# Retention and a mixture of experts on one core: weight pieces loaded and cast a block earlier, choices and gathers reordered

## The chip, the cores and the metric

One core of a Trainium2 chip runs the whole kernel as one program. The metric is device time in microseconds, the median of several runs. The engines are TensorE (PE), VectorE (DVE), ScalarE (ACT), GpSimd (POOL) and SyncE (SP); SP issues the plain transfers, POOL the indirect ones, and each engine works through its program in order, waiting on semaphores.

## The reference

Attention is a retention with a decay per head; its output is the input of a top-1 mixture of experts.

```python
gamma = 1.0 - 2.0 ** (-5.0 - np.arange(H))
for t in range(S):                       # B, H, S, D = 4, 8, 768, 64
    state = gamma * state + einsum('bhd,bhe->bhde', k[:, :, t], v[:, :, t])
    y[:, :, t] = scale * einsum('bhd,bhde->bhe', q[:, :, t], state)
x = y.transpose(0, 2, 1, 3).reshape(B * S, H * D)          # 3072 rows of 512
logits = normalized(x) @ normalized(expert_emb).T / tau    # 8 experts
e = argmax(logits); gate = softmax(logits)[e]
out = gate * (relu(x @ w1[e]) @ w2[e])                     # w1: 512 x 1024, w2: 1024 x 512
```

## The kernel before

The retention runs in 12 blocks of 256 positions (`m` from 0 to 11, `NM` is 12; three blocks make one batch). A block has scores q.k (L381), a mask on DVE (L401), products of q with the running state (`inter`, L444), products of the masked scores with v (`intra`, L444), and products that carry the state on (L415). In the same turn the next block is got ready: POOL scales k and q two blocks ahead (`scale_k` L344, `scale_q` L339), PE transposes them (L350, L368) and ACT copies the transposes out of PSUM (`kT` L355, `qT` L369). `take(m)` (L460, L463, ACT) copies a block's result out of the two `py` banks, of which there is one pair, so that the next block's `inter` must wait for it. DVE turns the result into rows (`rows_turn`, L468) and SP writes them to the scratch `xd` in DRAM (L475, four writes of 128 KB).

Beside this runs the routing. `logits_products` and `logits_rows` (L488, L496) give a block's logits; for a group of blocks (`GROUPS`) `sums` and `choose` find the expert of each row (L506 to L526, result `oh`), `add_counts` and `count` count rows per expert (L533 to L546), `ranks` gives each row its slot (L553 to L557, result `sloti`), and `place` writes a 16-word entry per row into the table `tbl` in DRAM, by one indirect transfer of POOL per 128 rows (L566). Block 8 is a group by itself, so that after block 9 the first 18 columns of the table (`NBE`) are known; `pad` (L582, L585) makes the later rows of expert 0 begin at slot 288. Then `early_slots` (L602, SP) loads the first 288 entries of expert 0, POOL turns their indices to integers (L590) and gathers the rows into `xge` (L596) in block 10. Block 9's rows and the next weight loads on SP are held until this gather has landed.

Expert weights come in pieces of 512 KB, eight per expert (`load_piece`, into one of four `raw` buffers); the first four pieces of expert 0 are each four transfers of 128 KB (L192), the others one (L194, L198). `split_cast` casts a piece on ACT into its high part (L219), and the function it gives back computes the low part on DVE (L224). In the kernel before, pieces 0 and 1 are loaded at the end of block 8, 2 and 3 in block 9, 4 and 5 in block 10; pieces 0 and 1 are cast ahead of block 9's `take`, 2 and 3 at the start of block 10.

After block 11 expert 0 runs on its early rows (`run`, L237, first layer), while the last group is counted, sorted and placed, the late entries of expert 0 are loaded (L937) and its late rows gathered into `xr0` (L596; the trace calls it `xr`), and PE transposes them (L1094). The other experts follow, each with its own gathers, first layer (L237) and second layer (L1024, L1072). The order on every engine is the order in which the code calls these functions. Where a transfer must come later than its data would allow, `after` adds a dependence.

Of the kernel before, what the change touches and what calls it, by code (L numbers as in the profile page):

```python
# [15 lines left out]
I32 = mybir.dt.int32  # L16
# [34 lines left out]
NBE = 2 * 9  # L51
SW = 16
FILL = 512
LOADS = (8, 8)
STRIDE = 3200
NOV = (NT - OV + P - 1) // P
NONE = 2 * NT
# [48 lines left out]
def retention_moe(ctx: ExitStack, tc: tile.TileContext, q, k, v, emb, tau, w1, w2, const, const16, out):  # L106
# [392 lines left out]
    def span(g):  # L499
        return slice(2 * GROUPS[g][0], 2 * GROUPS[g][-1] + 2)  # L500
# [72 lines left out]
    def run_all(*gs):  # L573
        gs = list(gs)
        while gs:
            gs = [g for g in gs if next(g, gs) is not gs]
# [10 lines left out]
                op0=ALU.is_gt, op1=ALU.add)  # L587

    def indices(p, e, c):
        nc.gpsimd.tensor_scalar(out=gi[:p, e, c], in0=tb[:p, e, c, 0], scalar1=float(NT - 1), scalar2=None, op0=ALU.min)  # L590

    def tokens(p, e, c):
        nc.gpsimd.tensor_copy(out=si[:p, e, c], in_=tb[:p, e, c, 1])

    def gather(xr, n, j, e, at, rows_=NT):
        return nc.gpsimd.indirect_dma_start(  # L596
            out=xr[:n, j, :], out_offset=None, in_=xd[:rows_, :],
            in_offset=bass.IndirectOffsetOnAxis(ap=gi[:n, e, at:at + 1], axis=0),
            bounds_check=rows_ - 1, oob_is_err=False)

    def early_slots():
        nc.sync.dma_start(out=tb[:, 0, :3], in_=tbl[:3 * P, :2 + NE].rearrange("(j p) o -> p j o", p=P))  # L602

    def early_gather():
        indices(P, 0, slice(0, 3))
        for j, n in EROWS:
            i = gather(xge, n, j, 0, j, NBE * P)
        tokens(P, 0, slice(0, 3))
        return i

# [125 lines left out]
    nc.gpsimd.memset(ze, 0.0)  # L736
    nc.gpsimd.memset(zt[:, :, 2 + NE:], 0.0)
    none = ap_.tile([P, NE * FILL // P * SW], F32, name="parts")
    nc.gpsimd.memset(none, float(NONE))
    for s in range(2):  # L740
        scale_q(0, s, nc.vector)
    transpose_q(0, 0)
# [19 lines left out]
    for m in range(NM):  # L762
        nxt = m + 1 < NM
        done = last_of.get(m - 1)
        if waiting is not None:
            pr = count(waiting)
            if span(waiting).stop == NBE:
                pad()
            run_all(ranks(waiting, pr))
            ready += range(span(waiting).start, span(waiting).stop)  # L770
        py_of(m)
        if m == NM - 2:
            first, lows = lows, [split_cast(), split_cast()]
            for u in range(2):
                spread_v(m + 1, u)

# [5 lines left out]
        if m == NM - 2:  # L782
            place(ready)
            ready = []
        if m == 0:
            for j in (*load_q(2), load_k(2)):
                after(j, i)
            nc.sync.dma_start(out=cst2, in_=const[:, _C1:])
            nc.sync.dma_start(out=tri, in_=const16)

        if m + 2 < NM:
            for s in range(2):
                after(scale_k(m + 2, s), i)
            for s in range(2):
                after(scale_q(m + 2, s), i)
        if m == 2:
            nc.gpsimd.tensor_copy(out=zt[:, :, :2], in_=C("ids").rearrange("p (n o) -> p n o", o=2))
        place(ready[:n])
        del ready[:n]
        if m == NM - 3:  # L800
            load_piece()
            load_piece()
        if m == NM - 2:
            early_slots()
            gathered = early_gather()
# [3 lines left out]
        if m == 0:  # L809
            state(0)  # L810
            state_copy(0)
            state_sums(0)
            intra(0, 0)
            intra(0, 1)
            transpose_k(1, 0)
            i = transpose_k(1, 1)
            after(load_v(2), i)
            inter(0)
            transpose_q(1, 0)
            i = transpose_q(1, 1)  # L820
            for j in (*load_q(3), load_k(3), load_v(3)):
                after(j, i)
            state(1)
            state_copy(1)
            state_sums(1)
        else:
            inter(m)
            if nxt:
                i = state(m + 1)
                state_copy(m + 1)  # L830
                if m + 3 < NM:
                    after(load_k(m + 3), i)
            if m == 2:
                after(nc.sync.dma_start(
                    out=tbl.rearrange("(e s) c -> e (s c)", e=NE)[:, :FILL * SW].rearrange("e (p x) -> e p x", p=P // NE),
                    in_=none), i)
            for i in () if m < 3 else (0, 1, 2) if m == 3 else (m - 1,):
                logits_rows(i, logits_products(i))
            if nxt:
                state_sums(m + 1)  # L840
                spread_v(m, 1, nc.vector.tensor_copy)
                transpose_k(m + 1, 0)
                transpose_q(m + 1, 0)
                i = transpose_q(m + 1, 1)
                if m + 3 < NM:
                    after(load_v(m + 3), i)
                transpose_k(m + 1, 1)
                rows(m - 1, gathered if m == NM - 2 else None)
                if m == NM - 2:
                    for low in first:  # L850
                        low()
                    load_piece(gathered)
                    load_piece(gathered)
                if done is not None:
                    z = sums(done)
                    run_all(choose(done, z))
                    run_all(add_counts(done))
                intra(m, 0)
                intra(m, 1)
            else:  # L860
                for low in lows:
                    low()
                intra(m, 0)
                z = sums(done)
                run_all(choose(done, z))
                run_all(add_counts(done))
                intra(m, 1)
                ps = [turn_rows(xge, EROWS, kt, bank(f"pst{kt}")) for kt in range(2)]
                pr = count(done)
                run_all(ranks(done, pr))  # L870
                place(range(span(done).start, span(done).stop))
        waiting = done
        if m == NM - 3:
            lows = [split_cast(), split_cast()]
        take(m)
        if m < NM - 2:
            spread_v(m + 1, 0)
        if m < 3:
            next(emb_steps)
        if m == NM - 1:  # L880
# [51 lines left out]
    for _ in range(9):  # L932
        next(sort_steps)
        run(1)
    load_expert(1)
    load_expert(2)
    nc.sync.dma_start(out=tb[:, 0, 3], in_=tbl[EARLY:CAPS[0], :2 + NE])  # L937
    slots(1)
    slots(2)
    run(10)  # L940
    split()
    run(12)
    split()
    for j, n in EROWS:
        square(xge, n, j, j)
    run(12)
    split()
    for _ in range(4):
        load_piece()
    run(DF)  # L950
    ctxa.close()
    turn_of[:] = ["b2", "b3"]
# [124 lines left out]
    yt0 = mp.tile([P, NXC, KT, Q], F32, name="yt", bufs=2)  # L1077
    og0 = mp.tile([P, NG, DM], F32, name="og", bufs=2)
    xr0 = mp.tile([P, 1, DM], F32, name="xr0")
    indices(P, 0, slice(3, 4))  # L1080
    gather(xr0, P, 0, 0, 3)
    indices(P, 1, slice(0, NG))
    gather_rows(1)
    tokens(P, 0, slice(3, 4))
# [183 lines left out]
    with ExitStack() as cx:  # L1268
# [3 lines left out]
        def expert_rows(e, i):  # L1272
# [7 lines left out]
            nc.sync.dma_start(out=mt, in_=tbl[ds(i * P + (e * STRIDE + OV), P), :])  # L1280
            g1 = op.tile([P, 1], I32, name="g1")
            s1 = op.tile([P, 1], I32, name="s1")
            nc.vector.tensor_scalar(out=g1, in0=mt[:, :1], scalar1=float(NT - 1), scalar2=None, op0=ALU.min)
            nc.vector.tensor_copy(out=s1, in_=mt[:, 1:2])
            xg = op.tile([P, 1, DM], F32, name="xg")
            nc.gpsimd.indirect_dma_start(
                out=xg[:, 0, :], out_offset=None, in_=xd[:, :],
# [23 lines left out]
        with tc.If(any_over > 0):  # L1311

            none = op.tile([P, SW], F32, name="none")
            nc.gpsimd.memset(none, float(NONE))
            nx = op.tile([P, NE], F32, name="nx")
            nc.vector.scalar_tensor_tensor(out=nx, in0=C("order"), scalar=float(STRIDE), in1=cnt, op0=ALU.mult, op1=ALU.add)
            nxi = op.tile([P, NE], I32, name="nxi")
# [36 lines left out]
```

## Time and profile before

| what | before |
|---|---|
| median of 3 runs | 403.92 us (402.48 to 404.23) |
| the profiled execution | 404.24 us, its span 402.5 us |
| PE busy | 386.1 us, 96% of the span |
| DVE, ACT, POOL busy | 254.1, 213.4, 150.9 us |
| granted clock of PE, mean | 0.997 |
| moved by DMA | 88.41 MB, 220 GB/s in the mean |

The span runs from the first to the last instruction; times in the rows below are microseconds from its start. A row of an order of time gives start, duration, engine, line, operation and tiles, and in brackets the idle time in front of it and what ended that. A count behind a tile (x32) means so many instructions merged into one row. "Idle" is worth time only on an engine that the end waits for.

### The profile page before, as it was taken

How to read it: one execution, taken by the hardware profiler on the slowest of the kernel's cores; microseconds unless marked ns; L12 is line 12 of the kernel's file. 1: busy time of each engine (PE TensorE's matmuls, PEld its weight loads, DVE VectorE, ACT ScalarE, POOL GpSimd, SP SyncE). 2: the span in 40 equal slices, each digit the busy share in tenths (PEclk: the TensorE clock that was granted, in tenths of full speed). 3: DMA queues.
4: the chain of work that ended last, by engine and by line, in shares of the span. 5: the costliest groups of instructions: out<-in, count | busy, mean ns of one | idle time of the engine just before them, and what ended most of it. 6: DMA issues, size and time to landing. Idle time of an engine off the chain costs nothing.

```text
span 402.5 us, 9525 instructions
## 1 busy us (share of the span) xinstructions
PE 386.1 (96%) x3646; PEld 355.2 (88%) x3646; DVE 254.1 (63%) x539; ACT 213.4 (53%) x378; POOL 150.9 (37%) x171
## 2 busy tenths in 40 slices
PE   6999999999899999999999999999999999999993
PEld 3998788887779978999999999999889889999972
DVE  5497867877889638854863864757456456485400
ACT  3575557565945356555544736725665445463410
POOL 2575487687445522402502611420371062001131
PEclk9999999999999999999999999999999999999998
DMA  7899979889448779589879797787888977933121
GB/s 228 262 287 254 277 225 280 235 229 260 104 130 258 234 263 265 161 267 249 266 223 247 241 302 175 246 277 221 236 273 298 190 240 225 246 122 107 31 99 54
DMA packets 88479, 88.41 MB, mean 220 GB/s; under 512 B 10803, under 2 KB 66995, under 8 KB 88424
## 3 DMA queue, kind: packets, MB, share of 16 engines
q1 hardware_dynamic: 83176, 74.60, 65.4%
q0 software_dynamic: 5072, 13.05, 9.6%
q8 instruction: 30, 0.49, 0.5%
q14 instruction: 25, 0.20, 0.2%
q10 hardware_dynamic: 176, 0.07, 0.1%
HBM read 65.01 MB, written 18.79 MB: 208 GB/s over the span
## 4 chain that ended last, share of the span: by engine, by line
PE 62%; DMA 15%; DVE 7%; issue 5%; SPq 5%; POOL 2%; ACT 2%; POOLq 0%; DVEq 0%
PE pst L237 10%; PE b L237 8%; PE py L1024 8%; PE py L237 8%; PE b L1024 5%; DMA xd<-x 5%; PE pst L1024 4%; PE b L1072 4%; PE py L1072 4%; DMA wlo<-in_k_dram 3%; SPq L1036 2%; DVE x L468 2%; PE b L381 2%; DMA xr<-xd,gi 2%; SPq L475 2%
## 5 line engine op out<-in xcount | busy, mean ns | idle before, releaser
L224 DVE TENSOR_TENSOR wlo<-raw,whi 128x1024 fp32r<-128x1024 f32 x64 | 77.8, 1218 | 23.2 <-ACT whi L219 18.3
L1054 POOL DMA_INDIRECT out_dram<-og,si x28 | 29.3, 1047 | 119.0 <-ACT og L1047 84.2
L219 ACT CAST whi<-raw 128x1024 fp32r<-128x1024 f32 x64 | 66.3, 1044 | 4.7 <-DMA raw<-in_moe_w_dram 4.6
L596 POOL DMA_INDIRECT xr<-xd,gi x25 | 29.3, 1171 | 17.5 <-issue 15.1
L401 DVE TENSOR_TENSOR pm<-b,mask 128x512 f32<-128x512 f32 x48 | 29.8, 681 | 8.9 <-PE b L381 8.9
L344 POOL TENSOR_TENSOR hl<-wlo,cst 128x512 f32<-128x512 f32 x22 | 22.6, 1049 | 31.5 <-DMA wlo<-in_k_dram 17.4
L237 PE MATMUL pst<-xl,whi 128*128 128x380 f32 (+7 forms) x96 | 32.1, 335 | 0.0
L237 PE MATMUL pst<-xh,whi 128*128 128x380 f32 (+7 forms) x96 | 32.0, 334 | 0.0
L237 PE MATMUL pst<-xh,wlo 128*128 128x380 f32 (+7 forms) x96 | 32.0, 333 | 0.0
L1005 DVE STREAM_TRANSPOSE xt<-xg 128x384 f32<-128x384 f32 (+1 forms) x28 | 15.7, 578 | 25.8 <-DMA xg<-xs 25.7
L263 POOL TENSOR_TENSOR r<-r,half 128x4 f32<-128x4 f32 (+1 forms) x9 | 8.9, 991 | 54.1 <-DVE r L262 54.1
L566 POOL DMA_INDIRECT tbl<-zt,sloti x24 | 24.2, 1009 | 12.6 <-issue 5.4
L243 ACT ACTIVATE hh<-pst 128x380 fp32r<-128x380 f32 (+7 forms) x24 | 11.6, 485 | 31.6 <-PE pst L237 31.6
L381 PE MATMUL b<-qT,kT 64*128 64x128 f32 x384 | 24.9, 279 | 2.4 <-ACT kT L355 1.5
L1006 ACT CAST xh<-xt 128x408 fp32r<-128x408 f32 (+6 forms) x28 | 14.2, 510 | 24.1 <-DVE xt L1005 23.8
L237 PE MATMUL b<-xh,whi 128*128 128x408 f32 (+7 forms) x80 | 26.7, 334 | 0.0
L237 PE MATMUL b<-xl,whi 128*128 128x408 f32 (+7 forms) x80 | 26.7, 333 | 0.0
L237 PE MATMUL b<-xh,wlo 128*128 128x408 f32 (+7 forms) x80 | 26.6, 332 | 0.0
L237 PE MATMUL py<-xh,whi 128*128 128x288 f32 (+7 forms) x80 | 26.3, 329 | 0.0
L237 PE MATMUL py<-xh,wlo 128*128 128x288 f32 (+7 forms) x80 | 26.2, 328 | 0.0
L237 PE MATMUL py<-xl,whi 128*128 128x288 f32 (+7 forms) x80 | 26.2, 327 | 0.0
L381 PEld LDWEIGHTS b<-qT,kT 64*128 64x128 f32 x384 | 22.5, 188 | 3.9 <-ACT kT L355 2.8
(220 smaller groups left out, 1044.2 us busy)
## 6 DMA issues: line engine op xcount, KB each, us to landing
raw<-in_moe_w_dram SPq DMA_DIRECT2D x60, 512.0 KB, 4.4
whi<-in_q_dram SPq DMA_DIRECT2D x24, 256.0 KB, 4.0
xd<-x SPq DMA_DIRECT2D x48, 128.0 KB, 4.2
wlo<-in_k_dram SPq DMA_DIRECT2D x11, 512.0 KB
xs<-xr SPq DMA_DIRECT2D x6, 768.0 KB, 4.8
whi<-in_v_dram SPq DMA_DIRECT2D x6, 512.0 KB
wlo<-in_v_dram SPq DMA_DIRECT2D x6, 512.0 KB, 6.0
xg<-xs SPq DMA_DIRECT2D x16, 192.0 KB, 4.6
```

What stands on the lines that cost most here:

```text
L219: nc.scalar.copy(out=hv, in_=rv)
L224: eng.tensor_tensor(out=lv, in0=rv, in1=hv.bitcast(F32), op=ALU.subtract)
L237: nc.tensor.matmul(acc[:, :w], a[:, f], x[:, kt, cols], start=(n == 0), stop=(n == 3 * KT - 1))
L344: return eng.tensor_tensor(out=ks_r[:, m % 3, s, h], in0=kin[m % 3][:, h, s], in1=w[:, h], op=ALU.mult)
L381: nc.tensor.matmul(psc[a][:, j], kTs[m][a * D:(a + 1) * D, j, u].rearrange("p s c -> p (s c)"), q_cols(m, a, j, u), start=True, stop=True, ...
L401: o.append(nc.vector.tensor_tensor(out=pm, in0=psc[a], in1=w, op=ALU.mult))
L566: i = nc.gpsimd.indirect_dma_start(out=tbl[:, :], out_offset=bass.IndirectOffsetOnAxis(ap=sloti[:, n:n + 1], axis=0), in_=zt[:, n], in_off ...
L596: return nc.gpsimd.indirect_dma_start(out=xr[:n, j, :], out_offset=None, in_=xd[:rows_, :], in_offset=bass.IndirectOffsetOnAxis(ap=gi[:n, ...
L1005: nc.vector.transpose(out=xt[:, :n], in_=xgs[e][:, :n, kt * Q:(kt + 1) * Q])
L1024: nc.tensor.matmul(acc[:, :c], a[:, f], x[:, kt, :c], start=(n == 0), stop=(n == 3 * FT - 1))
L1054: i = nc.gpsimd.indirect_dma_start(out=out[:, :], out_offset=bass.IndirectOffsetOnAxis(ap=si[:n, e, j:j + 1], axis=0), in_=og[:n, j, :], i ...
L1072: nc.tensor.matmul(acc[:s, :], x[:, kt, at], a, start=(n == 0), stop=(n == 3 * FT - 1))
```

## The change

Eight things change; `NM - 2` is block 10, `NM - 3` block 9, `NM - 4` block 8.

1. Pieces 0 and 1 are loaded at the end of block 7 and pieces 2 and 3 at the end of block 8, none in block 9.
2. Pieces 0 and 1 are cast at the end of block 8, behind its `take` and a copy of v, and 2 and 3 ahead of block 9's `take`, none in block 10. The low part of piece 0 stands ahead of block 9's logits on DVE, that of piece 1 where both stood.
3. In block 9 the choice and counts of group 3 stand ahead of the row transposes, and in block 10 the ranks ahead of `pad`.
4. q of block 11 is scaled in block 10 behind the placements, not in block 9 ahead of them.
5. The table's first two words are integers, written as such.
6. The gathers of expert 0 take their offsets from the loaded table itself; its index steps (L590) are gone, and entries without a row are out of bounds and skipped. `xr0` is cleared by a memset first.
7. Two of the four pieces that stood behind expert 0's last casts are loaded earlier, ahead of the loads of the late table.
8. The same integer entries are used in the code for overflowing experts, which does not run here.

```diff
--- before.py
+++ after.py
-LOADS = (8, 8)
+LOADS = (7, 7, 8, 8)
...
-    def gather(xr, n, j, e, at, rows_=NT):
+    def gather(xr, n, j, e, at, rows_=NT, idx=None):
...
-            in_offset=bass.IndirectOffsetOnAxis(ap=gi[:n, e, at:at + 1], axis=0),
+            in_offset=bass.IndirectOffsetOnAxis(ap=gi[:n, e, at:at + 1] if idx is None else idx, axis=0),
...
     def early_gather():
-        indices(P, 0, slice(0, 3))
         for j, n in EROWS:
-            i = gather(xge, n, j, 0, j, NBE * P)
+            i = gather(xge, n, j, 0, j, NBE * P, tb[:n, 0, j, :1].bitcast(I32))
         tokens(P, 0, slice(0, 3))
...
             pr = count(waiting)
+            run_all(ranks(waiting, pr))
             if span(waiting).stop == NBE:
                 pad()
-            run_all(ranks(waiting, pr))
...
         if m == NM - 2:
-            first, lows = lows, [split_cast(), split_cast()]
             for u in range(2):
                 spread_v(m + 1, u)
...
         if m == NM - 2:
             place(ready)
             ready = []
+            for s in range(2):
+                scale_q(m + 1, s)
...
-            for s in range(2):
+            for s in range(2 if m < NM - 3 else 0):
                 after(scale_q(m + 2, s), i)
...
-        if m == NM - 3:
-            load_piece()
-            load_piece()
...
+            if m == NM - 2:
+                lows.pop(0)()
             for i in () if m < 3 else (0, 1, 2) if m == 3 else (m - 1,):
                 logits_rows(i, logits_products(i))
...
+                if m == NM - 3:
+                    z = sums(done)
+                    run_all(choose(done, z))
+                    run_all(add_counts(done))
                 rows(m - 1, gathered if m == NM - 2 else None)
                 if m == NM - 2:
-                    for low in first:
-                        low()
+                    lows.pop(0)()
                     load_piece(gathered)
                     load_piece(gathered)
-                if done is not None:
+                if done is not None and m != NM - 3:
...
         if m == NM - 3:
-            lows = [split_cast(), split_cast()]
+            lows += [split_cast(), split_cast()]
         take(m)
         if m < NM - 2:
             spread_v(m + 1, 0)
+        if m == NM - 4:
+            lows = [split_cast(), split_cast()]
...
     load_expert(1)
+    load_piece()
+    run(10)
+    split()
+    load_piece()
     load_expert(2)
     nc.sync.dma_start(out=tb[:, 0, 3], in_=tbl[EARLY:CAPS[0], :2 + NE])
     slots(1)
     slots(2)
-    run(10)
-    split()
     run(12)
...
-    for _ in range(4):
-        load_piece()
+    load_piece()
+    load_piece()
...
     xr0 = mp.tile([P, 1, DM], F32, name="xr0")
-    indices(P, 0, slice(3, 4))
-    gather(xr0, P, 0, 0, 3)
+    nc.gpsimd.memset(xr0, 0.0)
+    gather(xr0, P, 0, 0, 3, idx=tb[:, 0, 3, :1].bitcast(I32))
```

On SP, from block 6's rows to block 8's rows (L475 rows, L327 q, L322 k and v of block 11, L192 chunks of the first pieces, L602 the early table), before:

```order
L475 DMA xd<-x 256x1x128 x4
L327 DMA whi<-in_q_dram 128x1x512 x2
L322 DMA wlo<-in_k_dram 128x8x128
L322 DMA wlo<-in_v_dram 128x8x128
L475 DMA xd<-x 256x1x128 x4
L192 DMA raw<-in_moe_w_dram 32x1024 x16
L475 DMA xd<-x 256x1x128 x4
```

and now:

```order
L475 DMA xd<-x 256x1x128 x4
L192 DMA raw<-in_moe_w_dram 32x1024 x8
L327 DMA whi<-in_q_dram 128x1x512 x2
L322 DMA wlo<-in_k_dram 128x8x128
L322 DMA wlo<-in_v_dram 128x8x128
L475 DMA xd<-x 256x1x128 x4
L192 DMA raw<-in_moe_w_dram 32x1024 x8
L475 DMA xd<-x 256x1x128 x4
```

The first eight chunks moved ahead of the loads for block 11; the second eight stay between block 7's and block 8's rows.

On ACT, from the copy of v behind block 8's `take` to block 10's copies of v (L219 casts, L460 and L463 block 9's `take`), before:

```order
L394 COPY vs<-wlo 64x512 x2
L422 COPY tB<-pst_1579 128x256
L355 COPY kT<-b_1830 128x8x64
L369 COPY qT<-b_1838 128x512
L369 COPY qT<-b_1844 128x512
L355 COPY kT<-b_1850 128x8x64
L219 CAST whi<-raw 128x1024 x2
L460 COPY yT<-py_1719 128x4x128
L463 COPY yT<-py_1720 64x4x128 x2
L394 COPY vs<-whi 64x512 x2
L219 CAST whi<-raw 128x1024 x2
L394 COPY vs<-wlo 64x512 x4
```

and now:

```order
L394 COPY vs<-wlo 64x512 x2
L219 CAST whi<-raw 128x1024 x2
L422 COPY tB<-pst_1589 128x256
L355 COPY kT<-b_1834 128x8x64
L369 COPY qT<-b_1842 128x512
L369 COPY qT<-b_1848 128x512
L355 COPY kT<-b_1854 128x8x64
L219 CAST whi<-raw 128x1024 x2
L460 COPY yT<-py_1735 128x4x128
L463 COPY yT<-py_1736 64x4x128 x2
L394 COPY vs<-whi 64x512 x2
L394 COPY vs<-wlo 64x512 x4
```

Two casts moved from block 10 to the end of block 8; two still stand ahead of block 9's `take`, and these are now pieces 2 and 3.

On POOL, from block 9's scaling to the early gather (L344 scale_k, L339 scale_q of block 11, L566 placements, four of block 9's and the two of group 3), before:

```order
L344 TENSOR_TENSOR hl<-wlo,cst_60 128x512 x2
L339 TENSOR_TENSOR hh<-whi,cst_60 128x8x64 x2
L566 DMA tbl<-zt,sloti 25600x16 x6
L590 TENSOR_SCALAR gi<-tb 128x3
L596 DMA xge<-xd,gi 128x512 x2
L596 DMA xge<-xd,gi 32x512
```

and now:

```order
L344 TENSOR_TENSOR hl<-wlo,cst_60 128x512 x2
L566 DMA tbl<-zt,sloti 25600x16 x6
L339 TENSOR_TENSOR hh<-whi,cst_60 128x8x64 x2
L596 DMA xge<-xd,tb 128x512 x2
L596 DMA xge<-xd,tb 32x512
```

The scaling of q moved behind the six placements, and the index step is gone.

## Rows read from the trace of the kernel before

**Rows 1.** The page, its first part: busy time, share of the span and instructions.

```profile
PE 386.1 (96%) x3646; PEld 355.2 (88%) x3646; DVE 254.1 (63%) x539; ACT 213.4 (53%) x378; POOL 150.9 (37%) x171
```

**Rows 2.** Busy time by stretches: PE, PEld, DVE, ACT, POOL; clock, DMA share, GB/s.

```profile
85.00:120.00 35.00, 31.66 (x538) 25.81 (x534) 28.79 (x74) 24.32 (x42) 20.21 (x21) 1.00 0.66 173
...
200.00:280.00 80.00, 80.00 (x449) 80.00 (x448) 50.63 (x102) 42.52 (x74) 19.61 (x21) 1.00 0.81 245
```

**Rows 3.** PE in order of time, block 10, block 11 and the late transposes.

```profile
99.59 0.17 PE L535 MATMUL b<-oh,tri 128*128 128x16 f16 x1 [0.67 <-DVE oh L526]
...
102.47 1.51 PE L444 MATMUL py<-qT,s 64*64 64x128 f32 x30
...
106.01 1.04 PE L368 MATMUL b<-ident,hh 128*128 128x128 f32 x8
...
107.41 1.97 PE L444 MATMUL py<-pm,vs 128*64 128x128 f32 x32
110.83 2.06 PE L381 MATMUL b<-qT,kT 64*128 64x128 f32 x32 [1.45 <-ACT kT L355]
...
116.67 1.16 PE L614 MATMUL pst<-ident,xge 128*128 128x128 f32 x6
...
143.47 0.66 PE L1094 MATMUL b<-ident,xr 128*128 128x128 f32 x4 [0.99 <-DMA xr<-xd,gi]
```

**Rows 4.** ACT in order of time, end of block 9 and block 10.

```profile
100.22 1.05 ACT L219 CAST whi<-raw 128x1024 fp32r<-128x1024 f32 x1 [0.98 <-DMA raw<-in_moe_w_dram]
101.17 0.58 ACT L460 COPY yT<-py 128x512 f32<-128x512 f32 x1
...
104.24 2.00 ACT L219 CAST whi<-raw 128x1024 fp32r<-128x1024 f32 x2
106.14 2.50 ACT L394 COPY vs<-wlo 64x512 f32<-64x512 f32 x4
```

**Rows 5.** SP's transfers in order of time: start and time to issue.

```profile
84.10 1.88 SPq L327 DMA_DIRECT2D whi<-in_q_dram  x2
86.07 0.54 SPq L322 DMA_DIRECT2D wlo<-in_k_dram  x1
...
89.08 3.19 SPq L475 DMA_DIRECT2D xd<-x  x4
92.31 8.33 SPq L192 DMA_DIRECT2D raw<-in_moe_w_dram  x16
...
116.19 2.52 SPq L475 DMA_DIRECT2D xd<-x  x4
...
134.06 2.18 SPq L194 DMA_DIRECT2D raw<-in_moe_w_dram  x4
```

**Rows 6.** Issue to landing: weight chunks (90 to 104), then the early gathers.

```profile
DMA to landing us min/median/max: 3.9/4.0/4.1
...
DMA to landing us min/median/max: 3.4/3.4/3.4
```

**Rows 7.** The chain that ended last: start, duration, what.

```profile
89.08 5.29 DMA xd<-x
94.39 2.94 DMA raw<-in_moe_w_dram
...
135.37 8.05 DMA xr<-xd,gi
```

**Rows 8.** POOL in order of time, blocks 9 and 10 and the late table.

```profile
92.53 2.04 POOL L344 TENSOR_TENSOR hl<-wlo,cst 128x512 f32<-128x512 f32 x2 [1.80 <-DMA wlo<-in_k_dram]
...
103.18 0.97 POOL L566 DMA_INDIRECT tbl<-zt,sloti  x1 [0.30 <-issue]
108.89 0.95 POOL L590 TENSOR_SCALAR gi<-tb 128x3 int32<-128x3 f32 x1 [4.74 <-DMA tb<-tbl]
...
133.98 1.12 POOL L590 TENSOR_SCALAR gi<-tb 128x1 int32<-128x1 f32 x1 [5.57 <-DMA tb<-tbl]
```

**Rows 9.** DVE in order of time, block 10.

```profile
105.65 0.45 DVE L496 STREAM_TRANSPOSE parts<-b 128x256 f32<-128x256 f32 x1 [1.63 <-PE b L488]
```

More of the change, by code (lines that the diff above doesn't have):

```diff
@@ L589, in indices @@
     def indices(p, e, c):
-        nc.gpsimd.tensor_scalar(out=gi[:p, e, c], in0=tb[:p, e, c, 0], scalar1=float(NT - 1), scalar2=None, op0=ALU.min)
+        nc.gpsimd.tensor_scalar(out=gi[:p, e, c], in0=tb[:p, e, c, 0].bitcast(I32), scalar1=float(NT - 1), scalar2=None, op0=ALU.min)
     def tokens(p, e, c):
-        nc.gpsimd.tensor_copy(out=si[:p, e, c], in_=tb[:p, e, c, 1])
-    def gather(xr, n, j, e, at, rows_=NT):
+        nc.gpsimd.tensor_copy(out=si[:p, e, c], in_=tb[:p, e, c, 1].bitcast(I32))
+    def gather(xr, n, j, e, at, rows_=NT, idx=None):
         return nc.gpsimd.indirect_dma_start(
             out=xr[:n, j, :], out_offset=None, in_=xd[:rows_, :],
-            in_offset=bass.IndirectOffsetOnAxis(ap=gi[:n, e, at:at + 1], axis=0),
+            in_offset=bass.IndirectOffsetOnAxis(ap=gi[:n, e, at:at + 1] if idx is None else idx, axis=0),
             bounds_check=rows_ - 1, oob_is_err=False)
@@ L738, in retention_moe @@
     none = ap_.tile([P, NE * FILL // P * SW], F32, name="parts")
-    nc.gpsimd.memset(none, float(NONE))
+    nc.gpsimd.memset(none.bitcast(I32), NONE)
     for s in range(2):
@@ L793, in retention_moe @@
                 after(scale_k(m + 2, s), i)
-            for s in range(2):
+            for s in range(2 if m < NM - 3 else 0):
                 after(scale_q(m + 2, s), i)
         if m == 2:
-            nc.gpsimd.tensor_copy(out=zt[:, :, :2], in_=C("ids").rearrange("p (n o) -> p n o", o=2))
+            nc.gpsimd.tensor_copy(out=zt[:, :, :2].bitcast(I32), in_=C("ids").rearrange("p (n o) -> p n o", o=2))
         place(ready[:n])
         del ready[:n]
-        if m == NM - 3:
-            load_piece()
-            load_piece()
         if m == NM - 2:
@@ L1282, in expert_rows @@
             s1 = op.tile([P, 1], I32, name="s1")
-            nc.vector.tensor_scalar(out=g1, in0=mt[:, :1], scalar1=float(NT - 1), scalar2=None, op0=ALU.min)
-            nc.vector.tensor_copy(out=s1, in_=mt[:, 1:2])
+            nc.vector.tensor_scalar(out=g1, in0=mt[:, :1].bitcast(I32), scalar1=float(NT - 1), scalar2=None, op0=ALU.min)
+            nc.vector.tensor_copy(out=s1, in_=mt[:, 1:2].bitcast(I32))
             xg = op.tile([P, 1, DM], F32, name="xg")
@@ L1313, in retention_moe @@
             none = op.tile([P, SW], F32, name="none")
-            nc.gpsimd.memset(none, float(NONE))
+            nc.gpsimd.memset(none.bitcast(I32), NONE)
             nx = op.tile([P, NE], F32, name="nx")
```

## The prediction

> **What bounds the kernel now.** I read the page first: TensorE (PE) is busy for 386.1 us of the span of 402.5 us [rows 1]. The table by stretches says where the rest lies. Once the experts run, only PE counts: 80.00 us busy in the 80 us from 200 to 280, while from 85 to 120 it is busy for 31.66 of 35 us [rows 2]. With the 0.99 us at 143.47 [rows 3] that makes 3.34 + 0.99 = 4.3 us, 1.1% of the time, and this is all that a change to blocks 8 to 11 and to the first expert can win. So each part is judged by whether it shortens one of PE's waits there or puts another into PE's program.
>
> PE's own order of time in blocks 10 and 11 [rows 3] is the skeleton. Block 10's counts wait 0.67 us for DVE's `oh`. Its products with the state (L444, from 102.47) are stretched to 1.51 us, because they write the banks that ScalarE's (ACT) `take` of block 9 (L460 and L463, from 101.17) is emptying [rows 4]. Its last products end at 107.41 + 1.97 = 109.38, and block 11's scores start at 110.83, after 1.45 us of waiting for ACT's copy of kT. ACT is late because its casts of the first weight pieces stand ahead of block 9's take and wait for their transfers; the second runs at 100.22 [rows 4].
>
> **The weight loads (the term that decides).** The change puts eight chunks of 128 KB ahead of block 11's q, k and v, and eight behind block 7's rows. SyncE (SP) took 8.33 us to issue sixteen, 0.52 each [rows 5]. It came to q at 84.10; now chunks go out until 88.3, q (1.88) until 90.2, k and v (0.54 each) until 91.2, the rows (3.19) until 94.4 and the second eight until 98.6, the last of them issued at 98.0. A chunk landed 4.0 us after its issue [rows 6], so the last lands at 102.0, and its cast (1.05) frees ACT at 103.1. SP may be held as well: a chunk was issued at 94.39, just when a row write issued at 89.08 had landed after 5.29 us [rows 7]. The last of block 7's four row writes now goes out at 93.6 and lands at 98.9; a chunk held for it lands at 102.9 and frees ACT at 104.0. Between 103.1 and 104.0 I take 103.4 for the start of the take, nearer to the end with the measured landing. It was 101.17.
>
> From the start of the take to block 10's end PE needed 109.38 - 101.17 = 8.2 us, and that work stays: block 11's scores could start at 111.6. ACT no longer adds to it. Before, it went from the take's start to 104.24 with the copies of y and v, and then through two casts (2.00 us) and four more copies of v (2.50) [rows 4]. Without the casts it is free 3.07 + 2.50 = 5.6 us after the take's start, at 109.0; kT and qT, which took it from 108.64 to 110.83, then end at 111.2. So the wait of 1.45 us goes, but the later take eats it: 111.6 in place of 110.83, **+0.8 us**.
>
> **GpSimd (POOL) and what is queued behind its wait.** k of block 11 was issued at 86.07, and POOL had idled for 1.80 us when it came at 92.53 [rows 5, 8], 6.4 us later. Issued at 90.2 it comes at 96.6. POOL used to run scale_k and scale_q (four of 1.02 us) and then six placements up to 103.18 + 0.97 = 104.15 [rows 8], the placements in 7.5 us. Now: scale_k to 98.7, placements to 106.2, and scale_q last, to 108.3. PE's transposes of q began at 106.01, 3.4 us ahead of block 10's end [rows 3]; from 108.3 that end is 111.7. The two delays run side by side and cost once, but neither covers the other's failure: with an early take, q still holds PE to 111.7; with early k, the take does.
>
> The early gather needs the last placement. Its table was at POOL 5.71 us after the placement's start, the index step took 0.95 [rows 8], and block 9's rows, which SP holds back until the gather has landed, went out at 116.19 [rows 5], 6.35 us after the index step. The last placement now starts at 105.2, the table is there at 110.9, the index step is gone, and the gather lands at 117.3. PE used it at 116.67 and now wants it at 117.5. Cover of 0.2 us, cost 0; earlier ranks do not help here, since POOL's queue and not DVE sets the placements.
>
> **Smaller edits, at nothing.** The choice ahead of the row transposes and the pad behind the ranks take away 0.67 us in front of block 10's scores, but the products behind those scores wait for the take. One low part ahead of block 9's logits lies where DVE idled for 1.63 us [rows 9], and PE's longer wait for the take covers the rest. The integer tables only reinterpret bits. The memset of the late rows lies in POOL's 5.57 us of waiting for the table [rows 8].
>
> **The late gather.** PE waits 0.99 us at 143.47 [rows 3] for a gather that was issued at 135.37 and took 8.05 us [rows 7], beside four weight pieces of 512 KB issued at 134.06 to 136.24 [rows 5]. The early gathers, with nothing else moving, took 3.4 [rows 6]: (8.05 - 3.4) / 4 = 1.2 us a piece, an estimate from these rows. Two of the four pieces now go ahead of the table's load. They cost SP 2 x 0.55 us in front of it, and their bytes at most 2 x 1.2; I take 1.0 of that. The table, at POOL at 133.98, comes at 136.1. The index step (135.37 - 133.98 = 1.4 us) is gone, so the gather starts at 136.1 and with two pieces beside it takes 3.4 + 2.4 = 5.8: it is there at 141.9, ahead of PE at 142.5. The wait goes if this holds and stays if it doesn't; I take **-0.8 us** between -0.99 and 0.
>
> A rule speaks against this term. The Trainium skill (DMA: Bandwidth & Descriptors, Queues, rings and completion order) says that a DMA engine takes turns between the queue rows that have work, a packet at a time, so that a gather shares with queued loads and does not stand behind them. By it the count of pieces in front hardly matters and the sum is +0.8. The 8.05 against 3.4 us fits either reading; no row here separates them.
>
> **Sum.** +0.8 - 0.8 = 0 on the profiled execution of 404.24, which stands 0.3 us above the median of 403.92. Both give **404.0, no change**; 0.5%, 2.0 us, is about what a measurement of this kernel can tell from no change.
>
> **The rivals.**
> *The loads hold ACT longer (slower, 0.20).* SP's transfers wait for older ones to land, as the chunk at 94.39 did. The second eight now stand behind k, v and four row writes that themselves queue behind 1 MB of chunks. If that stretches the row writes' 5.29 us by 2, the last chunk goes out at 100.9 and lands at 104.9, the take starts at 106.0, PE idles behind block 10's scores, and block 11 starts at 106.0 + 8.2 = 114.2: +3.4, less 0.8, gives 406.7. It decides once the last chunk lands after about 104.5. For it: 6.4 us for k and 5.29 for rows show queues that were full already. Against: a DMA share of 0.66 from 85 to 120 [rows 2] leaves room.
> *The loads fit into that room (faster, 0.12).* k is there at 92.5 as before, the placements end at 104.15 - 2.0, q is scaled by 104.2 and the last chunk lands by 99. Block 10 then ends 104.2 + 3.4 = 107.6 and block 11's scores follow: -3.2, and -0.8, gives 400.1. Against: SP's issue alone moves k by 4 us.
> *The late gather is no faster (0.13).* If it gets its share of the DMA engines whatever is queued, or if the two pieces delay the table by what they save, the 0.99 us stay: +0.8, 404.9, no change that can be told. The skill's rule above would make it so.
>
> **How the numbers follow.** The forecast has 0.55, the rivals 0.20, 0.12 and 0.13. Faster by over 0.5% is the second rival, 0.12, slower the first, 0.20; within 0.5% are the other two, 0.68. The range from 402.0 to 406.6 takes in the take's bounds, the gather's (0 and -0.99) and the near half of the first rival; it leaves out the far half of that one and most of the second, 0.2 in all.
>
> **What would show it.** Right: ACT casts the fourth piece at about 102 to 103 and block 9's take follows; POOL's wait for k ends at about 96.6 and scale_q at about 108; block 11's scores start near 111.6 with no wait for kT; the late gather lands before PE asks for it. Wrong: a take at 105 or later, with PE's products with the state waiting 3 us and more; or k at 93 and scores of block 11 at 108; or a wait for the late gather as long as it was.

## The result and the profile after

The change makes the kernel **slower: 409.40 us** in the median (408.66 to 411.65) against 404.08 us of the kernel before in the same comparison, a ratio of 1.0134 with an interval from 1.0103 to 1.0166. The forecast was 404.0 us. A ratio here is not the quotient of the two medians: it is worked out over the runs, without those more than 1.5% above the fastest of their kernel (one each in experiments 2 and 5, one of the kernel before). The profiled execution took 410.01 us, its span is 408.3 us against 402.5, and the mean granted clock is 0.984 against 0.997; in all four runs it was 0.983 to 0.985.

On the page of the kernel after, PE's busy time has grown by 3.8 us over [rows 1], with the same count of instructions:

```profile
PE 389.9 (95%) x3646; PEld 358.6 (88%) x3646; DVE 254.7 (62%) x539; ACT 213.7 (52%) x378; POOL 149.7 (37%) x170
```

The table by stretches says where (the columns are those of [rows 2]: PE, PEld, DVE, ACT, POOL, then the clock, the DMA share and GB/s):

```profile
95.00:100.00 5.00, 4.43 (x70) 3.85 (x68) 4.57 (x16) 1.76 (x4) 2.04 (x2) 1.00 0.84 218
100.00:105.00 5.00, 1.16 (x14) 0.96 (x14) 4.25 (x9) 1.04 (x1) 3.96 (x4) 1.00 0.98 246
105.00:110.00 5.00, 2.54 (x38) 2.14 (x40) 0.00 (x0) 4.52 (x7) 4.19 (x5) 0.51 0.31 77
110.00:115.00 5.00, 5.00 (x51) 4.07 (x47) 2.04 (x5) 2.68 (x6) 2.04 (x2) 0.50 0.14 23
```

PE stands almost still from 100 to 105 and has 2.54 us of work from 105 to 110; and from 105 to 115 its granted clock is a half, 1.2 in place of 2.4 GHz. Nothing like it is in the kernel before until the end of the span. PE in order of time, from the last products of block 9 to the scores of block 11, and then the late transposes (to be held against [rows 3]):

```profile
95.97 1.97 PE L444 MATMUL py<-pm,vs 128*64 128x128 f32 x32
...
100.10 1.16 PE L381 MATMUL b<-qT,kT 64*128 64x128 f32 x14 [0.67 <-DVE ex L583]
...
106.96 0.69 PE L444 MATMUL py<-qT,s 64*64 64x128 f32 x4 [5.71 <-ACT yT L460]
108.16 1.76 PE L444 MATMUL py<-qT,s 64*64 64x128 f32 x26 [0.50 <-ACT yT L463]
...
115.89 1.97 PE L444 MATMUL py<-pm,vs 128*64 128x128 f32 x32
117.79 0.38 PE L381 MATMUL b<-qT,kT 64*128 64x128 f32 x2
...
149.28 0.60 PE L1100 MATMUL b<-ident,xr 128*128 128x128 f32 x4
```

PE waits 5.71 us for block 9's `take` before the first products of block 10 with the state. Block 11's scores start at 117.79, not at 110.83, and there is no wait for kT and none for the late gather. ACT shows why the take is late [rows 4]:

```profile
91.16 2.00 ACT L219 CAST whi<-raw 128x1024 fp32r<-128x1024 f32 x2
...
103.18 1.04 ACT L219 CAST whi<-raw 128x1024 fp32r<-128x1024 f32 x1 [6.42 <-DMA raw<-in_moe_w_dram]
105.38 1.04 ACT L219 CAST whi<-raw 128x1024 fp32r<-128x1024 f32 x1 [1.16 <-DMA raw<-in_moe_w_dram]
106.33 0.58 ACT L460 COPY yT<-py 128x512 f32<-128x512 f32 x1
```

Pieces 0 and 1 are cast at 91.16 without a wait, but the casts of pieces 2 and 3 wait 6.42 and 1.16 us for their chunks. SP's transfers [rows 5], and then those around the late table:

```profile
83.19 5.94 SPq L192 DMA_DIRECT2D raw<-in_moe_w_dram  x8
90.59 0.54 SPq L322 DMA_DIRECT2D wlo<-in_k_dram  x1
...
91.86 6.57 SPq L475 DMA_DIRECT2D xd<-x  x4
98.48 3.87 SPq L192 DMA_DIRECT2D raw<-in_moe_w_dram  x8
...
137.56 1.00 SPq L194 DMA_DIRECT2D raw<-in_moe_w_dram  x2
139.28 0.34 SPq L945 DMA_DIRECT2D tb<-tbl  x1
...
141.06 1.22 SPq L194 DMA_DIRECT2D raw<-in_moe_w_dram  x2
```

The first eight chunks took 5.94 us to issue, the four row writes behind k and v 6.57 us in place of 3.19 us, and the last eight chunks were issued until 98.48 + 3.87 = 102.35. The last of the casts starts at 105.38, so the last chunk, issued at 101.9, had landed within 3.5 us. SP's load of the late table in the kernel before:

```profile
132.24 0.35 SPq L937 DMA_DIRECT2D tb<-tbl  x1
```

POOL after [rows 8]:

```profile
97.93 2.04 POOL L344 TENSOR_TENSOR hl<-wlo,cst 128x512 f32<-128x512 f32 x2 [8.07 <-DMA wlo<-in_k_dram]
...
107.77 2.05 POOL L339 TENSOR_TENSOR hh<-whi,cst 128x512 f32<-128x512 f32 x2
...
115.35 0.93 POOL L596 DMA_INDIRECT xge<-xd,tb  x1 [0.30 <-issue]
...
144.79 1.06 POOL L596 DMA_INDIRECT xr<-xd,tb  x1 [4.44 <-DMA tb<-tbl]
```

**Where the 5.8 us of the span are.** Executions of one kernel differ by a microsecond or two before block 9 already, so places are best counted from the start of block 9's last products: 95.97 here, and in the kernel before

```profile
96.84 1.97 PE L444 MATMUL py<-pm,vs 128*64 128x128 f32 x32
```

From there to block 11's scores it takes 21.82 us against 13.99, **+7.83**. From the scores to the late transposes it takes 31.49 against 32.64, -1.15, of which 0.99 is the wait for the gather that is gone. From the late transposes to the end both need 259.0. The earlier start gives 0.87: 7.83 - 1.15 - 0.87 = 5.8.

### The profile page after: what moved, and what is told of

Same layout as the page of the kernel before. It is cut to its first block, busy times and chain, and to the rows that moved or that the text cites. A ratio compares the mean times of both kernels' runs of the same rounds, so it can differ in the third digit from the quotient of the medians.

```text
span 408.3 us, 9523 instructions
## 1 busy us (share of the span) xinstructions
PE 389.9 (95%) x3646; PEld 358.6 (88%) x3646; DVE 254.7 (62%) x539; ACT 213.7 (52%) x378; POOL 149.7 (37%) x170
## 4 chain that ended last, share of the span: by engine, by line
PE 60%; issue 6%; POOL 3%; SPq 2%; DMA 2%; DVE 1%; POOLq 0%
PE pst L237 11%; PE b L237 9%; PE py L237 8%; PE py L1030 8%; PE b L1030 6%; PE pst L1030 6%; PE b L1078 4%; PE py L1078 4%; SPq L1042 2%; PE pst L1078 1%; POOL out_dram L1060 1%; POOL tbl L566 1%; DMA xd<-x 1%; PE b L1121 1%; PE py L1121 1%
## 5 line engine op out<-in xcount | busy, mean ns | idle before, releaser
L219 ACT CAST whi<-raw 128x1024 fp32r<-128x1024 f32 x64 | 66.3, 1043 | 7.6 <-DMA raw<-in_moe_w_dram 7.6
L344 POOL TENSOR_TENSOR hl<-wlo,cst 128x512 f32<-128x512 f32 x22 | 22.6, 1048 | 37.1 <-DMA wlo<-in_k_dram 22.8
L596 POOL DMA_INDIRECT xr<-xd,gi x24 | 28.1, 1172 | 17.2 <-DMA raw<-in_moe_w_dram 9.9
L566 POOL DMA_INDIRECT tbl<-zt,sloti x24 | 24.4, 1016 | 16.9 <-DVE sloti L557 9.4
```

The lines of the kernel that those rows point to most:

```text
L219: nc.scalar.copy(out=hv, in_=rv)
L344: return eng.tensor_tensor(out=ks_r[:, m % 3, s, h], in0=kin[m % 3][:, h, s], in1=w[:, h], op=ALU.mult)
L566: i = nc.gpsimd.indirect_dma_start(out=tbl[:, :], out_offset=bass.IndirectOffsetOnAxis(ap=sloti[:, n:n + 1], axis=0), in_=zt[:, n], in_off ...
L596: return nc.gpsimd.indirect_dma_start(out=xr[:n, j, :], out_offset=None, in_=xd[:rows_, :], in_offset=bass.IndirectOffsetOnAxis(ap=gi[:n, ...
```

## The experiments

Two theories stood at the start. **Casts:** the chunks of pieces 2 and 3 land late, ACT's casts hold the take, PE waits 5.7 us and then pays again at half clock. **GpSimd:** k of block 11 is late, the placements stand ahead of the scaling of q, and this would hold PE by itself. Ratios are to the kernel before, with the interval; "the stretch" is from block 9's last products to block 11's scores (13.99 us before, 21.82 after).

**1. The casts behind the take.**

```diff
+        take(m)
+        if m < NM - 2:
+            spread_v(m + 1, 0)
         if m == NM - 3:
             lows += [split_cast(), split_cast()]
-        take(m)
-        if m < NM - 2:
-            spread_v(m + 1, 0)
```

> The change with one edit: ACT's casts of the third and fourth weight piece stand behind block 9's take, not ahead of it. Take theory (ACT is held by those casts, whose chunks land late, and PE idles 5.71 us for the take and then runs 10.2 us at half clock): the take starts at about 98 in place of 106.33, the 5.71 us wait of the products with the state and the half-clock stretch behind it go; PE then waits for block 11's q, which GpSimd scales until 109.8, and block 11's scores start at about 113.2 in place of 117.79: 4.6 us less, about 405. GpSimd theory (k late, placements, q scaled last hold PE in any case): scores stay at 116 or later, 408 or more. If a wait for q of some 3 us drops the clock as the wait for the take did, 114.5 and 406.5.

Measured: 405.88 us, ratio 1.000 (0.997 to 1.003): the whole loss is back. ACT's `take` starts at 97.93. On PE:

```profile
96.79 1.97 PE L444 MATMUL py<-pm,vs 128*64 128x128 f32 x32
...
102.28 1.10 PE L444 MATMUL py<-qT,s 64*64 64x128 f32 x32
...
108.54 1.09 PE L368 MATMUL b<-ident,hh 128*128 128x128 f32 x8 [3.08 <-POOL hh L339]
...
113.51 2.06 PE L381 MATMUL b<-qT,kT 64*128 64x128 f32 x32
```

The products with the state no longer wait; the transposes of q do, 3.08 us, and the clock falls behind that wait too (0.70 from 110 to 115). The casts made the loss, and GpSimd's chain stands behind them as the next bound.

**2. The loads as before, all else of the change kept.**

```diff
-LOADS = (7, 7, 8, 8)
+LOADS = (8, 8)
...
+            first, lows = lows, [split_cast(), split_cast()]
...
+        if m == NM - 3:
+            load_piece()
+            load_piece()
```

> The change with its loads, casts and low parts put back as they were before, all else of it kept (choice ahead of the row transposes, ranks ahead of the pad, q scaled last, gathers straight from the table, integer tables, two pieces of expert 1 earlier). If the loads alone make the loss: block 11's scores at 111 or earlier, no stretch at half clock before the end, the wait of 0.99 us for the late gather gone, 402.9 to 403.5, equal to or up to 1 us below before. If scaling q last costs by itself (GpSimd): scores at 112 or later and 405 or more.

Measured: 404.94 us, ratio 0.9969 (0.9932 to 1.0007): the other edits lose nothing. In the profiled execution PE did not wait for the late gather, but block 11's scores came only at 113.75, because the clock fell to 0.50 from 105 to 110, behind two waits of 0.56 and 0.76 us for block 9's take:

```profile
105.00:110.00 5.00, 5.00 (x65) 4.07 (x61) 0.95 (x3) 4.87 (x7) 1.65 (x2) 0.50 0.26 59
```

That probably did not happen in each run: five of ten have a mean granted clock of 0.983 to 0.991, the other five 0.996 to 0.998. So the expected place of the scores, 111 or earlier, was missed in this execution; scaling q last is not what held them, since PE's transposes of q did not wait.

**3. The loads alone, on the kernel before** (the edits of experiment 2 the other way round).

> The kernel before with the new loads, casts and low parts alone. If the loads alone make the loss: take of block 9 at about 106, a wait of PE of 5 to 6 us, a stretch at half clock, block 11's scores at 117 to 118, the late wait of 0.99 us kept, 409.5 to 411. If the loss needs q scaled last too: scores at 114 or earlier, under 407.

Measured: 407.70 us, ratio 1.0088 (1.0056 to 1.0120). ACT:

```profile
103.27 1.04 ACT L219 CAST whi<-raw 128x1024 fp32r<-128x1024 f32 x1 [0.47 <-DMA raw<-in_moe_w_dram]
104.22 0.58 ACT L460 COPY yT<-py 128x512 f32<-128x512 f32 x1
```

The loads alone lose two thirds of it, less than expected. In this execution the row writes took 4.03 us to issue, not 6.57, so the take came 8.0 us after the start of block 9's last products (10.4 in the change, 4.3 before), and PE waited 1.18 us for it; the stretch is 16.15 us. The clock is 0.66 from 100 to 105; it fell ahead of that wait, behind 0.58 and 1.14 us of waiting for DVE: block 10's scores in front of it took 3.69 us, against 2.43 before the change. The wait for the late gather is there, 1.56 us. Scaling q last is not needed for the loss.

**4. Idle products in the wait.** 26 products of a tile of ones, whose result nobody reads, keep PE busy behind block 10's scores:

```diff
+        if m == NM - 2:
+            idle = pt_()
+            for _ in range(26):
+                nc.tensor.matmul(idle, ones, ones.unsqueeze(1).broadcast_to([P, 4, P]), start=True, stop=True)
```

> The change with 26 products of a tile of ones added (128x128 by 128x512, into a bank that nobody reads) behind block 10's scores, so that PE is busy in the wait for the take. They add work and use none of its results. If the half clock costs what the rows suggest (7.73 us from the products with the state to the last products of block 10, against 4.9 before): the stretch at half clock goes and block 11's scores start 2.5 to 3 us earlier, at about 115, 406.8. If the loss is the wait alone, the time stays at 409.4 or rises.

PE, and the stretches from 105 to 115:

```profile
97.16 1.97 PE L444 MATMUL py<-pm,vs 128*64 128x128 f32 x32
...
103.23 5.77 PE L782 MATMUL b<-ones 128*128 128x512 f16 x26 [0.21 <-DVE pm L401]
108.93 1.10 PE L444 MATMUL py<-qT,s 64*64 64x128 f32 x32
...
115.25 2.06 PE L381 MATMUL b<-qT,kT 64*128 64x128 f32 x32
```

```profile
105.00:110.00 5.00, 5.00 (x57) 2.69 (x57) 1.10 (x1) 4.58 (x8) 4.38 (x5) 1.00 0.30 75
110.00:115.00 5.00, 5.00 (x90) 4.36 (x85) 3.35 (x7) 4.45 (x8) 2.38 (x4) 1.00 0.20 47
```

The take is as late as in the change (106.26), PE starts its products with the state even later, and still the stretch is 18.09 us in place of 21.82: **of the 7.83 us the clock is worth 3.7 at least, and the wait 4.1 at most**. The 3.7 is a lower bound, because the idle products run on past the take: PE begins the products with the state 11.8 us after the start of block 9's last products, against 11.0 in the change. At the end little of this is left: 409.20 us over four runs, ratio 1.0103 (1.0024 to 1.0182), not to be told from the change's 1.0134. The profiled execution came to block 9's last products 1.2 us later than the change's, and 1.4 us are lost again behind the late transposes (260.5 us to the end, not 259.0), where PE now waits three times, 0.7 us in all, for the low parts of the next expert's rows (`xl`); the rest of that 1.4 stays open.

**5. q scaled ahead of the placements**, on the kernel of experiment 1.

```diff
-            for s in range(2):
-                scale_q(m + 1, s)
...
-            for s in range(2 if m < NM - 3 else 0):
+            for s in range(2):
```

> The kernel of the first experiment (casts behind the take) with one more edit: GpSimd scales block 11's q ahead of the six placements, as before the change, not behind them. In the first experiment PE waited 3.08 us for q and block 11's scores started at 113.51. GpSimd theory (the late k costs once more through q scaled last): the wait for q goes, block 11's scores start at 109.5 to 110.5; the placements and the early gather come about 2 us later, so PE then waits 2 to 3 us for the rows of the early gather, and the time gains 1 us at most over the first experiment. If the gather has more cover than that, the whole 3 us come back and the time is 402 to 403. If PE waits for kT instead (ACT has the two casts at 102.6 to 105.7 in front of it), scores at 112 or later.

Measured: 409.37 us, ratio 1.0082 (1.0044 to 1.0120), worse than experiment 1. The runs spread from 404.65 to 410.91 us, at mean clocks of 0.998 down to 0.979; the profiled one is the longest. PE:

```profile
111.52 2.06 PE L381 MATMUL b<-qT,kT 64*128 64x128 f32 x32 [1.33 <-ACT kT L355]
...
119.11 0.33 PE L613 MATMUL pst<-ident,xge 128*128 128x128 f32 x1 [1.69 <-DMA xge<-xd,tb]
121.32 0.47 PE L613 MATMUL pst<-ident,xge 128*128 128x128 f32 x1 [1.88 <-DMA xge<-xd,tb]
```

The stretch is 13.78 us, as short as before the change, but the early gather, whose first part is issued at 115.62, is now so late that PE waits 3.7 us for it, and the clock is 0.54 from 120 to 125 and 0.50 from 125 to 130. In this execution, with k late, POOL's order only chooses which of two waits PE gets; by the times the change's order, q last, was the better one. The expectation named the wait for the gather and missed the clock.

**6. The last eight chunks ahead of the row writes**, on the change.

```diff
-LOADS = (7, 7, 8, 8)
+LOADS = (7, 7)
...
+                if m == NM - 4:
+                    load_piece()
+                    load_piece()
                 rows(m - 1, gathered if m == NM - 2 else None)
```

> The change with one move: the third and fourth weight piece's eight chunks are issued ahead of block 7's four row writes, not behind them. Queue theory (the chunks land late because SP stands at the row writes, 6.57 us for four, each held until an older transfer has landed): the last chunk is issued by 97.5 and lands by 101.5, the take starts at 102 to 103 in place of 106.33, PE waits 1 to 2 us for it, and then q, scaled until about 109.8, holds block 11's scores at about 113: some 4 us less than the change. Bandwidth theory (the DMA engines, 0.84 to 0.98 busy from 90 to 105, can't deliver earlier whatever the order): the last chunk lands at 103 or later and the take starts at 105 or later, time within 1.5 us of the change.

Measured: 408.14 us, ratio 1.0071 (1.0038 to 1.0104). SP, ACT and PE:

```profile
91.58 7.82 SPq L192 DMA_DIRECT2D raw<-in_moe_w_dram  x8
```

```profile
103.21 0.58 ACT L460 COPY yT<-py 128x512 f32<-128x512 f32 x1
```

```profile
103.84 0.44 PE L444 MATMUL py<-qT,s 64*64 64x128 f32 x4 [1.76 <-ACT yT L460]
...
114.52 2.06 PE L381 MATMUL b<-qT,kT 64*128 64x128 f32 x32
```

The take starts 7.1 us after block 9's last products, against 10.4 in the change, and PE waits 1.76 us for it, as the queue theory had it. But SP took 7.82 us for these chunks, as it took 6.57 for the row writes in the change: it is held behind k and v whatever comes next. What the new order itself gained is less sure: with the change's order of loads the take came 10.4, 9.1 and 8.0 us after that start (the change, experiments 4 and 3), so between 0.9 and 3.3 us. That the chunk now has half a megabyte less in front of it would make 2.1 to 2.4 us at the 218 to 246 GB/s of the table, an estimate; that the bytes in front decide, and not the kind of transfer, fits but is not shown. The clock fell here too (0.57 from 105 to 110), and the scores came at 114.52 in place of 113.

**7. Expert 1's pieces moved, alone**, on the kernel before.

```diff
     load_expert(1)
+    load_piece()
+    run(10)
+    split()
+    load_piece()
     load_expert(2)
...
-    run(10)
-    split()
...
-    for _ in range(4):
-        load_piece()
+    load_piece()
+    load_piece()
```

> The kernel before with only expert 1's pieces moved: two of the four ahead of the table's load, two as far back as in the change. The late gather still has its index step. If the count of pieces beside the gather set its 8.05 us: gather 5 to 6 us, PE's wait of 0.99 us for it gone or under 0.3. If the index step (1.4 us) was the cause: the wait stays at 0.8 us or more.

Measured: 405.58 us, ratio 1.0015 (0.9983 to 1.0047). POOL gets the table 4.91 us after SP's load of it at 133.45, and the gather behind it is there before PE asks at 143.16:

```profile
139.58 1.14 POOL L596 DMA_INDIRECT xr<-xd,gi  x1 [0.99 <-DMA raw<-in_moe_w_dram]
```

That is under 3.6 us from issue to use, against 8.05 [rows 7], with the index step still there. The wait of 0.99 us is gone, but 1.1 us come back behind it, again with small waits for the low parts of the next expert's rows (0.6), and the time is the same.

**8. Loads as before, and the casts late.** On the kernel of experiment 2, the first two casts stand behind block 9's take and its copies of v, the other two behind block 10's take:

```diff
-            first, lows = lows, [split_cast(), split_cast()]
+            first = lows
...
-        if m == NM - 3:
-            lows = [split_cast(), split_cast()]
         take(m)
         if m < NM - 2:
             spread_v(m + 1, 0)
+        if m == NM - 3:
+            lows = [split_cast(), split_cast()]
+        if m == NM - 2:
+            lows = [split_cast(), split_cast()]
```

> The kernel of the second experiment (loads as before, all else of the change) with its casts of weight pieces moved: the first two behind block 9's take and its copies of v, the other two behind block 10's take. Theory: the take of block 9 starts at about 98 (no chunk is waited for), PE's waits behind block 10's scores go and with them the stretch at half clock; q, scaled until about 105.8, and the last products of block 10 set block 11's scores, at 109 to 109.5; no wait for the late gather; about 400.5 to 402, 0.5 to 0.9% faster than before. If the later low parts and casts delay DVE or ACT in block 11: the early rows' transposes or the first expert's products wait for a piece, and it is no faster than before.

Measured: **401.87 us, ratio 0.9934 (0.9903 to 0.9964)**, faster than both kernels. ACT and PE:

```profile
99.47 0.59 ACT L460 COPY yT<-py 128x512 f32<-128x512 f32 x1 [0.35 <-PE py L444]
...
102.81 1.99 ACT L219 CAST whi<-raw 128x1024 fp32r<-128x1024 f32 x2
```

```profile
98.33 1.97 PE L444 MATMUL py<-pm,vs 128*64 128x128 f32 x32
...
106.38 1.09 PE L368 MATMUL b<-ident,hh 128*128 128x128 f32 x8 [0.26 <-POOL hh L339]
...
109.73 2.06 PE L381 MATMUL b<-qT,kT 64*128 64x128 f32 x32
```

The casts wait for nothing, PE waits 0.26 us for q and for nothing else up to block 11's scores, the stretch is 11.40 us, and the clock is full in it.

**9. The same, with expert 1's four pieces back where they were.** The late gather still reads its indices from the table.

> The fastest kernel so far (loads as before, casts late) with expert 1's four pieces put back where they were before; the late gather still reads its indices straight from the table, so only the index step is gone. If the index step alone made the wait of 0.99 us: no wait of PE for the late gather, and the small waits for expert 1's low parts (0.8 us at 158 to 161) gone too, 400.5 to 401.5. If the pieces made it: PE, which now reaches the late transposes at about 141, waits 1 to 2.5 us for the gather, which takes 7 us or more to land, 402.5 to 404.

Measured: 402.79 us, ratio 0.9975 (0.9948 to 1.0003). POOL, PE, and the landing of the gather (issues with KB and median us to landing):

```profile
131.76 1.83 POOL L596 DMA_INDIRECT xr<-xd,tb  x1 [0.93 <-DMA tb<-tbl]
```

```profile
140.65 0.63 PE L1101 MATMUL b<-ident,xr 128*128 128x128 f32 x4 [1.03 <-issue]
```

```profile
xr<-xd,tb POOLq DMA_INDIRECT x1, 8.8
```

Without the index step the gather is still not there: it takes 8.8 us, and PE waits 1.03 (its row names no releaser; 131.76 + 8.8 = 140.56 is when the gather lands). From SP's load of the table to these transposes it is 11.65 us without the index step, and 11.23 and 11.99 with it (the kernel before and experiment 10). So the pieces in flight set that wait, and the index step had no share in it that could be seen.

**10. The four casts late, on the kernel before**, and nothing else (the edit of experiment 8).

> The kernel before with only the four casts moved, as in the fastest kernel: the first two behind block 9's take, the others behind block 10's; nothing else of the change. The take then starts at about 98.5 in place of 101.17 and ACT no longer holds kT: block 11's scores at 108.5 to 109.5 in place of 110.83. If the late gather does not come earlier with them, PE's wait of 0.99 us for it grows to 2 or 2.5 and eats the gain: 403.5 to 404.5, the same as before. If it does, 402 to 403, 0.3 to 0.6% faster.

Measured: 403.43 us, ratio 0.9978 (0.9956 to 1.0001). The stretch is 12.17 us, 1.8 less than before, and PE then waits 2.03 us for the late gather. The profiled execution, 405.90 us, is the longest of twelve; another 2.3 us of it lie behind the late transposes, of which 1.4 are two waits for low parts of weights. The late casts and the moved pieces each buy next to nothing alone; together, with the change's other edits in experiment 8, they are worth 0.7%.

## Why the prediction was wrong

**The step that failed is the start of the take**: "Between 103.1 and 104.0 I take 103.4 for the start of the take". It came at 106.33, in an execution that was 0.9 us ahead at block 9. The mechanism was right: the take waits for the cast of the sixteenth chunk, and that chunk landed about as fast as forecast (3.5 us, not 4.0). What was mis-sized is SP's time to come to it. The step took SP's issue times from [rows 5], 0.52 us a chunk and 3.19 for the row writes. Measured were 5.94 us for the first eight chunks (not 4.2), 6.57 for the row writes, and an end of the issue at 102.35, not 98.6. It added issue times and took the DMA share of 0.66 [rows 2] for room. But that is a mean over 85 to 120, and the room in it lies behind 105 (the columns are those of the table above):

```profile
100.00:105.00 5.00, 4.80 (x101) 4.19 (x105) 3.63 (x11) 4.68 (x7) 3.21 (x4) 1.00 0.93 234
105.00:110.00 5.00, 4.38 (x57) 3.56 (x56) 4.29 (x8) 4.94 (x9) 0.95 (x1) 1.00 0.06 5
```

From 90 to 105, where the take is decided, the kernel before was already at 0.93 to 1.03. There the take waited for the eighth of sixteen chunks, now it waits for the sixteenth, with 1 MB more in front. At the 218 to 246 GB/s of the stretches from 95 to 105 that is 4.3 to 4.8 us, an estimate, against the 2.2 us that the prediction allowed. Counted from block 9's last products the take moved by 10.4 - 4.3 = 6.0 us in this execution, and by 3.7 to 4.8 in those of experiments 3 and 4 with the same order of loads.

**The second failure is "that work stays"**: 8.2 us from the take to block 11's scores. It was 117.79 - 106.33 = 11.5, because the clock was a half. The two make up the miss of block 11's scores: 117.79 - 111.6 = 6.2, of which 2.9 are the take and 3.3 the work behind it. This is why the first rival fell short as well. Its mechanism, ACT held by the loads because SP's transfers wait for older ones, is the one that happened. That its take at 106.0 is nearly exact is partly luck, since experiment 3 has it at 104.22 with the same order of loads; and it priced the rest at full clock and came to 406.7. The clock was in no term of the sum and in no rival.

**POOL** went as told and later: k at 97.93, not 96.6, q scaled until 109.8, not 108.3. That neither delay covers the other's failure held: with the take out of the way q alone held PE (experiment 1).

**The smaller edits**: the 0.67 us in front of block 10's scores is gone and comes back inside them, as a wait for `pad`'s result at 100.10, in the shadow of the longer wait. Nothing else of them shows.

**The early gather** was covered, as told: its last part was issued at 115.35 and took 2.75 us in the chain of waits, and PE came later.

**The late gather** was right in its result: the 0.99 us went, and moving the pieces did it (experiments 7 and 9), with the index step of no weight. Its prices were not: with two pieces behind the table the gather was to take 5.8 us, and it took under 4.5 in the change, under 3.6 in experiment 7. The table paid for it: from its load to the gather's issue it took 5.51 us (139.28 to 144.79) against 3.13. So two things changed at once. The pieces beside the gather are two, not four; and the last of them was issued 2.9 us ahead of the gather (3.3 in experiment 7), where it used to go out 0.5 us behind the gather's start. Which of the two counts is not shown. The rule that was weighed against this term, the Trainium skill's (DMA: Bandwidth & Descriptors, Queues, rings and completion order) turns between queues, does not fit as it was read there, that the count of pieces hardly matters: 256 KB took 8.05 and 8.8 us beside four pieces of 512 KB and under 3.6 with two of them ahead of the table (experiment 7).

## What to carry to other kernels

When loads and casts move, ask of each consumer which transfer it now waits for and how many bytes stand ahead of that one; a queue's issue rate with room in it did not hold here with one more megabyte in front. Work that waits for DRAM does not belong ahead of a copy that frees a bank for TensorE, if that copy could go first. And price a wait of TensorE of some microseconds in two parts, the wait itself and the products behind it, which may run at half clock; here these were about 4.1 and 3.7 us.

## What the runs showed of the hardware

That the clock falls in the middle of a run was not expected: 0.51 and 0.50 from 105 to 115, from the midst of PE's wait of 5.71 us on. With PE kept busy in the same wait it stayed at 1.00 (experiment 4). The Trainium skill (TensorE: Matmul & The Clock Gate, HAM oscillation — how this bites in real kernels) describes this: products behind a wait for data start at the lower clock. The traces agree, and also show the fall behind waits of 3.08 us (experiment 1), 1.76 and 0.76 us (experiment 6), 0.58 and 1.14 us (experiment 3) and, in some runs of one kernel and not in others, 0.56 and 0.76 us (experiment 2), while the kernel before, with a wait of 1.45 us in that place, and experiment 10, with one of 2.03 us at 142.82, kept their full clock there. What decides between these is left open.

SP was held while older transfers were under way: whatever it had to issue behind k and v took 4.0 to 7.8 us in place of 3.2 (four row writes) and 4.2 (eight chunks, half of the 8.33), row writes and chunks alike (6.57 in the change, 4.03 in experiment 3, 7.82 in experiment 6). In experiment 6 the trace names what its chunks waited for longest, the landing of v, 2.4 us; in the change it names no transfer there.
